# Short SSM products that wait in the plan while many TensorE instructions were begun lately, and a new stretch ahead of the first exponential

## The chip, the cores and the metric

The kernel runs on one core of one Trainium2 chip. The metric is the device time of one execution in microseconds (us), the median of several runs. Engines are named as the profile names them: PE is TensorE (PEld its weight loads), DVE is VectorE, ACT is ScalarE, POOL is GpSimd, SP is SyncE, from which most transfers are issued.

## What is computed

Two independent layers on sequences of 2048 rows with 640 features; their outputs are joined along the features.

```python
def _A_ref(x, Lambda_re, Lambda_im, B_re, B_im, C_re, C_im, log_dt, Dskip):
    Lam = Lambda_re + 1j * Lambda_im
    dt = jnp.exp(log_dt)
    Lam_bar = jnp.exp(dt * Lam)
    B_bar = ((Lam_bar - 1.0) / Lam)[:, None] * (B_re + 1j * B_im)
    Bu = jnp.einsum("bld,pd->blp", x + 0j, B_bar)
    for t in range(L):
        h = Lam_bar[None, :] * h + Bu[:, t, :]
        hs.append(h)
    return 2.0 * jnp.einsum("blp,dp->bld", jnp.stack(hs, 1), C_re + 1j * C_im).real + x * Dskip

def _B_ref(x, wq, wk, wv, wo):            # 32 query heads of 20, one key and value head
    q = (x @ wq).reshape(B, S, 32, 20).transpose(0, 2, 1, 3)
    scores = jnp.einsum("bhqd,bkd->bhqk", q, x @ wk) * (20 ** -0.5)
    o = jnp.einsum("bhqk,bkd->bhqd", softmax(scores, axis=-1), x @ wv)
    return o.transpose(0, 2, 1, 3).reshape(B, S, 640) @ wo
```

The first layer is a state space model (SSM), a recurrence over time with a complex diagonal; the second is attention with 32 heads that share one key and one value head.

## The kernel before

**The program is planned when it is built.** `Schedule` holds a small model of the five engines. Each step is an `Op` with an engine, a planned duration, its dependencies and a priority. Whenever a modelled engine is free, `pick` takes the ready step with the lowest priority number, and the order in which steps were picked becomes each engine's instruction stream; `Emitter` adds the semaphore waits. A `gate` is a function that must be true for a step to be picked. Nothing of the planner runs on the chip, but each of its rules decides the fixed order there. A random seed (`SEEDS`) shifts the due places of the background tasks, and `STAGES` changes the planner's constants as tiles are filled.

**Attention.** The scores of one head and 512 queries against 128 keys make a tile, [128 keys, 512 queries]; 32 blocks of 64 tiles are 2048 tiles. PSUM has eight banks of [128, 512]: two groups of three (`SC`) and two single ones (`MB`). `fill` scores two or three tiles into an SC group, and one ACT exponential (L1530) turns two or three of them into bf16 probabilities in `PR`. If the third bank holds a tile of the other route, DVE takes it: a `TENSOR_SCALAR` to int16 (L867), an exponential by its bits, and three shifted copies of it by POOL (`int64_add`, L1858) or DVE; four value products with differently scaled values (`VS`) then stand for one. Such tiles (here: tiles of the DVE route) are also scored into MB banks when one is free. The two SC groups take turns: while ACT reads one, PE fills the other, which it may do once ACT and DVE have emptied it (`slot_last`). The value products (L1946) add up in one MB bank, `pvbank`.

**Background work** shares PE with that: query projections, output projections (`WO`), and the SSM: unit tasks (`xaT` with `BA`, `BT`), a scan on DVE, and the output products `y_task`, whose moving operand has 512 columns, or 128 for the last 128 features (`k == 4`) and for the skip term (`diagD`). `ride` hands these to PE in steps of up to 256 columns, each product as four matmuls on 32 columns of the array; `board` lets one product that is cut in row groups ride along with a score fill.

**Ahead of the first exponential.** x is loaded plainly for the first 1024 rows and transposed by PE (`turn`), and loaded transposed for the others (`XB`: pieces of 128-feature columns on SP, one of five, then three and two columns). `kv` makes the keys of each 512 rows on PE (L1162, with `wks`, the key weights repeated four times), the largest absolute key (L1168) and the scaled keys `KT`. `bound` makes the largest of all (L1194) and `M0`, a matrix that turns absolute queries into a bound on each query's scores; `qt_task` makes the first queries, the product with `M0`, and `QT` (L867). `attention` starts when all SC banks are free. `v_task` makes the values (L1218) and casts them (L1226).

**At the end** tiles of the DVE route are taken until `LAST` tiles before the end and copied by POOL until `POOL_LAST` tiles before it.

## Time and profile before

| what | us |
|---|---|
| median of 3 runs | 697.55 (697.17 to 698.18) |
| the profiled execution | 697.62 |
| its span, first to last instruction | 695.9 |
| start of the first exponential | 18.41 |
| end of the last exponential | 687.68 |
| PE, ACT, DVE, POOL busy | 683.2, 681.8, 637.0, 470.4 |

The profile is of one execution. A row of a timeline has the start, the length, the engine, the line, the operation with what it writes and reads, and how many instructions it joins; in brackets, the idle time just before it and what ended that. "issue" there means that no semaphore ended it. A row of the groups ends with the busy time, the mean of one in ns, and the idle time before the group. A row of windows has a stretch, then for PE, PEld, DVE, ACT and POOL the busy time and the number of instructions, the granted clock of TensorE as a share of full speed, and the share and rate of the transfers. A row of waits has who waited for whom, the total, how often, and the longest.

### The profile page before, as it was taken

What the parts mean: (1) busy time and instruction counts of PE and PEld (TensorE: products, weight loads), DVE (VectorE), ACT (ScalarE), POOL (GpSimd) and SP (SyncE); (2) the same over time, 40 slices, a digit from 0 to 9 for tenths busy, and PEclk for the clock granted to TensorE, in tenths of its full rate; (3) what the DMA queues carried; (4) which work ended last, traced back from release to release, by engine and by line L of the source; (5) the groups of instructions that cost most, each with busy time, mean ns of one, the idle gap of its engine ahead of it and who ended that gap; (6) DMA issues with size and microseconds to landing.
All of it is one profiled execution on the core that took longest, in us unless ns stands there. A gap on an engine that the chain in (4) does not pass through costs nothing.

```text
span 695.9 us, 27390 instructions
## 1 busy us (share of the span) xinstructions
PE 683.2 (98%) x11488; PEld 250.6 (36%) x11490; DVE 637.0 (92%) x1243; ACT 681.8 (98%) x703; POOL 470.4 (68%) x796
## 2 busy tenths in 40 slices
PE   8999999999999999999999999999999999999998
PEld 5322332334334333333433333334333332343335
DVE  7899999999999889999999999999999999977795
ACT  7999999999999999999999999999999999999996
POOL 4256666564587668767778777676776767788880
DMA  9659641211130111102110101131000001110001
GB/s 217 175 127 187 139 103 39 62 26 32 30 94 13 32 27 27 35 21 29 44 26 22 28 27 28 35 58 20 13 15 12 20 15 36 37 29 22 21 15 41
DMA packets 77591, 34.48 MB, mean 50 GB/s; under 512 B 58350, under 2 KB 77470, under 8 KB 77470
## 3 DMA queue, kind: packets, MB, share of 16 engines
q1 hardware_dynamic: 76650, 32.57, 20.3%
q8 instruction: 92, 1.51, 0.9%
q10 hardware_dynamic: 820, 0.16, 0.1%
q14 instruction: 29, 0.24, 0.1%
HBM read 11.53 MB, written 9.75 MB: 31 GB/s over the span
## 4 chain that ended last, share of the span: by engine, by line
PE 56%; ACT 42%; DVE 1%; issue 0%
ACT PR L1530 41%; PE MB L1946 21%; PE MB L800 14%; PE SC L1626 10%; PE MB L810 8%; PE MB L730 1%; DVE BIG L867 1%; PE SC L1162 1%; PE SC L726 1%; PE MB L726 0%; ACT L2197 0%; PE SC L730 0%; DVE pvsb L1925 0%; PE MB L1279 0%; DVE QT L867 0%
## 5 line engine op out<-in xcount | busy, mean ns | idle before, releaser
L1530 ACT ACTIVATE PR<-SC 128x1024 bf16<-128x1024 f32 (+1 forms) x678 | 666.6, 1131 | 4.5 <-PE SC L1626 3.3
L1858 POOL INT64_ADD BIG<-BIG x761 | 458.1, 617 | 198.1 <-DVE BIG L867 54.7
L867 DVE TENSOR_SCALAR BIG<-SC 128x512 int16<-128x512 f32 x560 | 376.2, 684 | 38.7 <-PE SC L1626 33.1
L1946 PE MATMUL MB<-BIG,VS 128*32 128x512 bf16 (+1 forms) x2468 | 269.8, 376 | 1.2 <-DVE pvsb L1925 0.9
L1626 PE MATMUL SC<-QT,KT 32*128 32x512 bf16 (+1 forms) x2073 | 265.3, 378 | 4.4 <-ACT PR L1530 1.8
L1946 PE MATMUL MB<-PR,VP 128*32 128x512 bf16 (+1 forms) x1495 | 222.3, 378 | 0.1
L1626 PEld LDWEIGHTS SC<-QT,KT 32*128 32x128 bf16 x2073 | 67.3, 91 | 133.8 <-ACT PR L1530 77.1
L1946 PEld LDWEIGHTS MB<-BIG,VS 128*32 128x32 bf16 x2468 | 68.5, 95 | 65.5 <-issue 41.4
L1946 PEld LDWEIGHTS MB<-PR,VP 128*32 128x32 bf16 x1495 | 55.1, 94 | 45.8 <-issue 33.0
L867 DVE TENSOR_SCALAR BIG<-BIG 128x1024 int16<-128x1024 int16 (+1 forms) x136 | 52.3, 419 | 0.9 <-PE MB L1946 0.4
L800 PE MATMUL MB<-CA,W 128*32 128x320 bf16 (+2 forms) x992 | 51.4, 299 | 0.4 <-DVE BIG L2366 0.4
L810 PE MATMUL MB<-xaT,BT 32*128 32x256 bf16 x192 | 37.1, 273 | 0.0
L800 PE MATMUL MB<-CT,W 128*32 128x512 bf16 (+1 forms) x640 | 36.0, 302 | 0.6 <-issue 0.6
L800 PE MATMUL MB<-xaT,BA 128*32 128x256 bf16 x800 | 31.8, 275 | 0.0
L810 PE MATMUL MB<-diagD,xaT 32*128 32x128 bf16 x320 | 31.3, 217 | 0.0
L810 PEld LDWEIGHTS MB<-diagD,xaT 32*128 32x128 bf16 x320 | 17.7, 92 | 29.1 <-ACT PR L1530 17.7
L800 PEld LDWEIGHTS MB<-CA,W 128*32 128x32 bf16 x992 | 22.8, 96 | 14.2 <-issue 5.7
L800 PE MATMUL MB<-xaT,BT 128*32 128x256 bf16 x608 | 26.2, 274 | 0.0
L2133 DVE CAST stg<-MB 128x512 bf16<-128x512 f32 x35 | 23.8, 680 | 1.8 <-PE MB L800 1.1
L862 DVE TENSOR_TENSOR prod<-MB,tab 128x1024 bf16<-128x1024 f32 x20 | 24.3, 1215 | 0.2
L867 DVE TENSOR_SCALAR BIG<-MB 128x512 int16<-128x512 f32 x35 | 23.8, 679 | 0.6 <-PE MB L1626 0.6
L2406 DVE TENSOR_TENSOR_SCAN g<-sc,hst,prod 128x256 bf16<-128x256 f32 x30 | 22.5, 749 | 0.0
(178 smaller groups left out, 502.4 us busy)
## 6 DMA issues: line engine op xcount, KB each, us to landing
out_dram<-stg SPq DMA_DIRECT2D x33, 128.0 KB, 2.0
qd<-BIG SPq DMA_DIRECT2D x20, 128.0 KB, 2.1
QT<-qd SPq DMA_DIRECT2D x28, 80.0 KB
OP<-pvsb SPq DMA_DIRECT2D x105, 20.0 KB
rdP<-recs SPq DMA_DIRECT2D x105, 20.0 KB
lbd<-BA SPq DMA_DIRECT2D x5, 320.0 KB, 2.7
CT<-in_B_x_dram SPq DMA_DIRECT2D x2, 640.0 KB, 5.3
BA<-in_A_B_re_dram SPq DMA_DIRECT2D x1, 800.0 KB, 7.5
```

The costliest lines, as they stand in the source:

```text
L726: r = e.matmul(out[32 * j:32 * j + 32], lhsT=lhsT[:, 32 * j:32 * j + 32], rhs=rhs, start=start, stop=stop, tile_position=(0, 32 * j), skip ...
L730: return lambda e: e.matmul(out, lhsT=lhsT, rhs=rhs, start=start, stop=stop, **kw)
L800: x = e.matmul(out[32 * j:32 * j + 32], lhsT=lhsT[:, 32 * j:32 * j + 32], rhs=rhs, start=start, stop=r.end is tag, tile_position=(0, 32 * ...
L810: return lambda e: e.matmul(out, lhsT=lhsT[at], rhs=rhs[at], start=start, stop=r.end is tag, tile_position=(32 * row, 0), skip_group_check ...
L862: return lambda e: e.tensor_tensor(out, a, b, op)
L867: return lambda e: e.tensor_scalar(out, a, s1, s2, op0=op0, op1=op1)
L1530: ex = self.act(lambda e: e.activation(dst, t[:, 0:512 * n], ACT.Exp, scale=1.0 / UNIT), 0.8333 * 512 * n + 64, table="exp", deps=[op], re ...
L1626: r = e.matmul(out[:, bank.off + lo:bank.off + lo + n], lhsT=p.KT[32 * j:32 * j + 32, 128 * c:128 * c + 128], rhs=p.QT[32 * j:32 * j + 32, ...
L1858: op.fns.append(lambda e: e.int64_add(words(dst), words(src), add))
L1946: r = e.matmul(bank.tensor[32 * j:32 * j + 32, bank.off + at:bank.off + at + n], lhsT=v[:, c, 0:32], rhs=rhs[:, lo:lo + n], start=first an ...
L2133: ev = self.dve(lambda e: e.tensor_copy(st, bank.ap), 645, deps=[prev], reads=[bank.key], writes=[key], prio=self.EV, gate=(lambda: last.e ...
L2406: o = self.dve(lambda e, ri=ri, init=init: e.tensor_tensor_scan(p.g[:, u, ri, :], rdec, p.prod[:, 1, 0, ri, :], init, ALU.mult, ALU.add), ...
```

## The change

Two things are added to the planner, one stretch is rewritten, and the plan is drawn anew.

**A gate on short products.** Every PE step that is begun is noted with its number of instructions (two for each entry in its list, eight for a ridden product, which is four matmuls with four weight loads). A ridden step whose moving operand has at most 128 columns may be picked only if fewer than `FETCH` = 220 instructions were begun in the last `SUPPLY` = 3400 planned ns; else it is asked again 130 ns later.

```diff
+    def issued(self, span):
+        while self.issues and self.issues[0][0] < self.t - span:
+            self.issues.popleft()
+        return sum(n for _, n in self.issues)
...
+            self.issues.append((self.t, op.per * len(op.fns)))
...
+    SUPPLY, FETCH = 3400.0, 220.0
...
-                         load=n, writes=[bank.key], hook=hook, gate=lambda: bool(r.steps))
+                         load=n, writes=[bank.key], hook=hook, gate=lambda: bool(r.steps) and (
+                             r.steps[0][0][0][2].shape[-1] > 128 or self.s.issued(self.SUPPLY) < self.FETCH or bool(self.s.at(self.s.t + 130.0))))
+            op.per = 8
```

On PE, within an output task with 128 columns of the SSM (`CT`, `CA` and `diagD` are its weights, `W` the states; SC<-QT,KT is a score fill, MB<-PR,VP and MB<-BIG,VS are value products), before:

```order
L810 MATMUL MB<-diagD,xaT 128x128 x3
L800 MATMUL MB<-CT,W 32x128 x4
L800 MATMUL MB<-CA,W 32x128 x4
L800 MATMUL MB<-CT,W 32x128 x4
L800 MATMUL MB<-CA,W 32x128 x4
L800 MATMUL MB<-CT,W 32x128 x4
L800 MATMUL MB<-CA,W 32x128 x4
L800 MATMUL MB<-CT,W 32x128 x4
L800 MATMUL MB<-CA,W 32x128 x4
L810 MATMUL MB<-diagD,xaT 128x128
L1626 MATMUL SC<-QT,KT 128x512 x3
```

and with the change, in the same task:

```order
L820 MATMUL MB<-diagD,xaT 128x128 x3
L810 MATMUL MB<-CT,W 32x128 x4
L810 MATMUL MB<-CA,W 32x128 x4
L1992 MATMUL MB<-PR,VP 32x512
L1992 MATMUL MB<-BIG,VS 32x512 x5
L1992 MATMUL MB<-PR,VP 32x512
L1992 MATMUL MB<-BIG,VS 32x512
L820 MATMUL MB<-diagD,xaT 128x128
L1672 MATMUL SC<-QT,KT 128x512 x3
```

After eight short products two of them stand between two fills here, and eight value products of 512 columns in the place of the others.

**The third bank.** When the third bank of an SC group holds a tile that DVE will, in the plan, empty too late, the next fill of that group takes two tiles and does not wait for it (`third_limit`, `third_known`, `third_late`, and `skip` in `fill`).

```diff
+        if self.skip[i]:
+            n, third = min(n, 2), self.third[i]
+            self.n_skip += 1
...
-        self.slot_last[i] = [ex] + first
+        self.slot_last[i] = [ex] + first + ([third] if third is not None else [])
+        self.third[i] = first[0] if first else third
...
+        ex, other = self.slot_last[i][0], self.slot_last[1 - i][0]
+        return ex.start + ex.dur + (other.dur if other.eng == "act" else 0.0) - 522.0 + self.SKIP
```

**The stretch ahead of the first exponential.** The last key product is no longer cut in two halves. The transposed pieces are of five, four and one column. M0 is made in two steps: from the first three maxima on ACT, then, as the smaller (more negative) of that and the last one, on DVE. DVE instead of ACT copies `wks`; the keys of the first two row groups are scaled on DVE, the others on ACT. The value products wait for M0's product, in the third banks, and attention starts without waiting for these banks.

```diff
-    WKP, QUAD_KEYS, WKE = 0.9, 0, "a"
-    TURNED, KEYS = ("adada", "adada"), "adaa"
-    XB = ((2, 0, 5, 11250.0), (3, 0, 3, 12500.0), (3, 3, 5, 13400.0))
+    WKP, QUAD_KEYS, WKE = 0.9, 0, "d"
+    TURNED, KEYS = ("adada", "adada"), "ddaa"
+    XB = ((2, 0, 5, 11250.0), (3, 0, 4, 13350.0), (3, 4, 5, 14150.0))
...
-            m = self.dve(lambda e: e.tensor_reduce(out=p.mab[:, 5:6], in_=p.mab[:, 0:5], axis=AX.X, op=ALU.max), 120,
-            self.m0_op = self.dve(self.ts(p.M0[:], p.mask0[:], p.mab[:, 5:6], None, ALU.mult), 200, port=True,
+            m = self.act(lambda e: e.activation(p.M0[:].rearrange("p a b -> p (a b)"), p.mask0[:].rearrange("p a b -> p (a b)"), ACT.Copy,
+                                                scale=p.mab[:, 4:5]), 260,
+            yield lambda: 3 in self.red_op
+            self.m0_op = self.dve(lambda e: e.scalar_tensor_tensor(out=p.M0[:], in0=p.mask0[:], scalar=p.mab[:, 3:4], in1=p.M0[:],
+                                                                   op0=ALU.mult, op1=ALU.min), 250, port=True,
...
-                           gate=lambda: self.lively(self.V_BY[tb // 3]))
+                           gate=lambda: (tb > 1 or self.m_first is not None and self.m_first.start is not None and (tb == 0 or self.tile_n > 0)) and self.lively(self.V_BY[tb // 3]))
...
-        mine = [b for _, bs in self.slots for b in bs]
+        mine = [b for _, bs in self.slots for b in bs[:-1]]
```

On PE, from the key products (SC<-BIG,wks) to the first scores, before; MB<-BIG,wqp are the first queries, MB<-PR keeps PE busy, MB<-BIG,M is the product with M0, SC<-wvr,BIG are the values, and the one row SC<-BIG is a product that rides ahead of the first scores:

```order
L1279 MATMUL MB<-BIG,wqp 128x512 x5
L1162 MATMUL SC<-BIG,wks 128x512 x8
L1162 MATMUL SC<-BIG,wks 128x256 x4
L730 MATMUL MB<-PR 128x512
L1218 MATMUL SC<-wvr,BIG 128x20 x20
L730 MATMUL MB<-PR 128x512 x2
L730 MATMUL MB<-BIG,M 32x512 x4
L1218 MATMUL SC<-wvr,BIG 128x20 x20
L730 MATMUL MB<-PR 128x512 x2
L810 MATMUL SC<-BIG 128x512
L1626 MATMUL SC<-QT,KT 128x512 x4
```

and with the change:

```order
L1294 MATMUL MB<-BIG,wqp 128x512 x5
L1171 MATMUL SC<-BIG,wks 128x512 x10
L737 MATMUL MB<-PR 128x512 x5
L737 MATMUL MB<-BIG,M 32x512 x4
L1235 MATMUL SC<-wvr,BIG 128x20 x20
L1672 MATMUL SC<-QT,KT 128x512 x4
```

Both groups of value products stood ahead of the first scores, with the rider; now one group does, behind M0's product, and the first scores have no rider.

**The plan.** `SEEDS` goes from 169732 to 531817, some constants of `STAGES` change, `LAST` goes from 12 to 16 and `POOL_LAST` from 14 to 29. On PE, the last rows of the program (SC<-BT,pvsb and SC<-WO,OP are parts of the last output projection), before:

```order
L726 MATMUL SC<-BT,pvsb 32x128 x16
L726 MATMUL MB<-BT,pvsb 32x512 x4
L726 MATMUL SC<-BT,pvsb 32x512 x8
L726 MATMUL SC<-WO,OP 32x512 x16
L726 MATMUL SC<-BT,pvsb 32x512 x8
```

and with the change:

```order
L733 MATMUL SC<-WO,OP 32x512 x8
L733 MATMUL SC<-BT,pvsb 32x128 x16
L733 MATMUL MB<-BT,pvsb 32x512 x4
L733 MATMUL SC<-WO,OP 32x512 x8
L733 MATMUL SC<-BT,pvsb 32x512 x8
```

Eight of the sixteen products of the last step stand ahead of the last value rows now.

129 lines of the change are left out of this document (76 added, 53 removed).

## The prediction

> **What bounds the kernel.** I read the page first: the busy shares, then the group of the exponentials.
>
> ```profile
> span 695.9 us, 27390 instructions
> PE 683.2 (98%) x11488; PEld 250.6 (36%) x11490; DVE 637.0 (92%) x1243; ACT 681.8 (98%) x703; POOL 470.4 (68%) x796
> L1530 ACT ACTIVATE PR<-SC 128x1024 bf16<-128x1024 f32 (+1 forms) x678 | 666.6, 1131 | 4.5 <-PE SC L1626 3.3
> ```
>
> TensorE (PE) and ScalarE (ACT) are both at 98%. A busy PE is a modelled figure, so I ask ACT: 678 exponentials, with only 4.5 us of idle time before them. Then the groups kept apart by shape, and ACT's timeline in order of time, in which a row ends where ACT waited visibly (a row bears the shape of its first instruction and counts both shapes).
>
> ```profile
> L1530 ACT ACTIVATE PR<-SC 128x1024 bf16<-128x1024 f32 x579 | 544.7, 1068 | 4.3 <-PE SC L1626 3.3 <-PE MB L1626 0.3 <-PE MB L1946 0.2
> L1530 ACT ACTIVATE PR<-SC 128x1536 bf16<-128x1536 f32 x98 | 141.6, 1505 | 0.1
> 18.41 185.56 ACT L1530 ACTIVATE PR<-SC 128x1024 bf16<-128x1024 f32 x183 [1.81 <-PE SC L1626]
> 204.13 133.17 ACT L1530 ACTIVATE PR<-SC 128x1024 bf16<-128x1024 f32 x136 [0.15 <-PE MB L1626]
> 337.93 35.60 ACT L1530 ACTIVATE PR<-SC 128x1024 bf16<-128x1024 f32 x37 [0.63 <-PE SC L1626]
> 373.70 132.75 ACT L1530 ACTIVATE PR<-SC 128x1024 bf16<-128x1024 f32 x137 [0.17 <-PE MB L1626]
> 506.64 19.42 ACT L1530 ACTIVATE PR<-SC 128x1024 bf16<-128x1024 f32 x20 [0.20 <-PE SC L1626]
> 526.30 46.90 ACT L1530 ACTIVATE PR<-SC 128x1024 bf16<-128x1024 f32 x48 [0.24 <-PE SC L1626]
> 573.37 108.38 ACT L1530 ACTIVATE PR<-SC 128x1024 bf16<-128x1024 f32 x112 [0.17 <-PE MB L1946]
> 682.14 5.54 ACT L1530 ACTIVATE PR<-SC 128x1024 bf16<-128x1024 f32 x5 [0.39 <-PE SC L1626]
> 687.05 0.63 ACT L1530 ACTIVATE PR<-SC 128x512 bf16<-128x512 f32 x1
> 511.75 9.29 ACT L1530 ACTIVATE PR<-SC 128x1024 bf16<-128x1024 f32 x10
> 520.79 1.18 ACT L1530 ACTIVATE PR<-SC 128x1024 bf16<-128x1024 f32 x1
> 167.86 8.25 ACT L1530 ACTIVATE PR<-SC 128x1536 bf16<-128x1536 f32 x6
> 169.19 1.55 ACT L1530 ACTIVATE PR<-SC 128x1536 bf16<-128x1536 f32 x1
> ```
>
> So the span is three pieces: 18.41 us until the first exponential, 669.27 us of exponentials (18.41 to 687.05 + 0.63), 8.2 us after them. The last four rows give the undisturbed step: ten 1024-column exponentials from 511.75 to 520.79 are 0.904 us each, a 1536-column one from 167.86 to 169.19 is 1.33 us. Then 579 x 0.904 + 98 x 1.33 + 0.63 = 654.4 us is what ACT must do, and 669.3 - 654.4 = 14.9 us is lateness of the scores, which sits in ACT's way whatever else is busy. Only part of it is visible as a gap: seven gaps after the first make 1.95 us, and each costs 0.16 more than it shows, since an exponential takes 1.068 but the next may begin after 0.904; that is 3.1 us. The other 11.8 us are delays too short to part two exponentials.
>
> **The work on ACT.** The order of the changed program holds 582 exponentials of two tiles, 99 of three and none of one, against 579, 98 and 1 (681 and 678 instructions): 1461 tiles instead of 1453. Eight tiles fewer take the VectorE route (587 against 595). The step per tile from the rows above is 1.33 - 0.904 = 0.426 us, so 3 x 0.904 + 1.33 - 0.48 = **+3.6 us** (the one-tile step is 0.904 - 0.426 = 0.48). Nothing hides that: ACT is the chain. VectorE and GpSimd are relieved, and neither bounds the span.
>
> **The stretch ahead of the first exponential.** The chain of waits there, from the timeline:
>
> ```profile
> 7.97 0.11 PEld L1162 LDWEIGHTS SC<-BIG,wks 128*128 128x128 bf16 x2 [1.05 <-ACT wks L1047]
> 9.74 1.41 PEld L1162 LDWEIGHTS SC<-BIG,wks 128*128 128x128 bf16 x8
> 9.97 1.67 PE L1162 MATMUL SC<-BIG,wks 128*128 128x512 bf16 x7 [0.16 <-issue]
> 14.26 0.34 PEld L1162 LDWEIGHTS SC<-BIG,wks 128*128 128x128 bf16 x4 [0.31 <-DMA BIG<-in_B_x_dram]
> 13.84 0.69 DVE L1168 TENSOR_REDUCE mab<-SC 128x1 f32<-128x512 f32 x1
> 15.91 0.29 DVE L866 TENSOR_SCALAR M<-mask,mab 128x128 bf16<-128x128 f32 x1
> 16.25 0.40 PE L730 MATMUL MB<-BIG,M 128*32 128x512 bf16 x4
> 16.70 0.81 DVE L867 TENSOR_SCALAR QT<-MB,lift 128x512 bf16<-128x512 f32 x1 [0.51 <-PE MB L730]
> 17.43 0.38 DVE L1226 CAST VP<-SC 128x80 bf16<-128x80 f32 x2
> 17.98 0.58 PE L1626 MATMUL SC<-QT,KT 32*128 32x512 bf16 x4
> ```
>
> The last transposed piece of x lands at 14.26; four short key products, two maxima, a maximum of maxima, M0 (ready 16.20), its product, QT (ready 17.51). The scores start only at 17.98, since a rider in their first operation needs the bank that the value cast empties (17.43 + 0.38 = 17.81). The change leaves one 512-column product behind the last landing, one maximum (0.69), and one operation that makes M0 from a part made earlier; and it runs the value products after M0's product, so that bank is free. From the landing: 14.26 + 0.38 product + 0.2 to VectorE + 0.69 + 0.06 + 0.29 (M0, by the row of the old M0) = 15.88; the product at 15.93, QT 16.38 to 17.19, scores 17.24, first exponential 0.43 later (as 17.98 to 18.41): 17.67, or -0.74 us. The other end is PE's own order: 24 whole key and query products at (1.67 - 0.38) / 6 = 0.215 us each now stand between the start of that run and the last maximum, so with a start at 9.74 as before the last begins at 9.74 + 23 x 0.215 = 14.69, 0.43 after the landing: -0.31 us. The start comes earlier, since wks is now copied on VectorE ahead of its casts and the 1.05 us wait for ACT shrinks; I take **-0.6 us**. The second transpose now brings four columns and the third one, with the same total behind the same queue, so I leave the last landing where it was; had the split of the pieces delayed it by 0.3, the term would be -0.4. The maximum for the rows that are loaded back, and the stores of q that now stand behind a transposed load on SP, are for blocks 2 and up: over a hundred tiles of exponentials (some 50 us) cover them.
>
> **The pauses of PE.** What the gate on short products is aimed at:
>
> ```profile
> 333.30:336.40 3.10, 3.10 (x154) 2.47 (x157) 2.97 (x8) 3.10 (x5) 1.85 (x4) 1.00 0.49 102
> 336.40:337.30 0.90, 0.28 (x24) 0.11 (x15) 0.85 (x2) 0.90 (x1) 0.57 (x1) 1.00 0.00 0
> 337.26 0.24 PE L800 MATMUL MB<-CT,W 128*32 128x128 bf16 x4 [0.61 <-issue]
> q8 instruction: 92, 1.51, 0.9%
> ```
>
> In 3.1 us PE began 154 products and 157 weight loads, then stood for 0.6 us waiting for nothing that a semaphore shows, and the exponential at 337.93 came 0.63 late. PE ran out of instructions: queue 8 brings them, 1.51 MB in 92 packets, 16 KB each. The changed order breaks such runs at about 110 products per four score fills (22 stretches above 130 before, 3 now). [...]
>
> The second cause is the third bank of a score group, which VectorE empties:
>
> ```profile
> PEld SC L1626 <- DVE BIG L867: 31.3, 77, 0.7
> 203.68 0.10 PEld L1626 LDWEIGHTS SC<-QT,KT 32*128 32x128 bf16 x3 [0.42 <-DVE BIG L867]
> 373.25 0.10 PEld L1626 LDWEIGHTS SC<-QT,KT 32*128 32x128 bf16 x3 [0.42 <-DVE BIG L867]
> 525.86 0.10 PEld L1626 LDWEIGHTS SC<-QT,KT 32*128 32x128 bf16 x3 [0.42 <-DVE BIG L867]
> ```
>
> Each of the last three stands half a microsecond ahead of a visible gap (204.13, 373.70, 526.30). The change fills two tiles there and leaves the third bank to VectorE. So of the seven gaps five are addressed: 0.63, 0.15, 0.17, 0.24 and, with the ending rearranged, 0.39; with 0.16 each that is 2.4 us. Of the 11.8 us of short delays I take a fifth (31.3 us of the idle time before score weights is VectorE's, against 77.1 that ends with ACT itself and is harmless): 2.1 us. Together **-4.5 us**, between 0 and about -9. The gate is the planner's: on the chip no instruction waits for longer, other products just stand where the short ones stood. What waits is the short products' bank, which their output task holds longer, so fewer tiles of the VectorE route find one (28 instead of 35 are scored into such banks); that price is in the +3.6.
>
> **The end.** After the last exponential the chain goes through this:
>
> ```profile
> 690.14 0.42 DVE L862 TENSOR_TENSOR pvsb<-pvsb,SC 128x256 bf16<-128x256 bf16 x1 [0.54 <-PE SC L730]
> 691.50 1.03 PE L726 MATMUL SC<-WO,OP 128*32 128x512 bf16 x16
> 693.02 0.60 ACT L2126 ACTIVATE PR<-SC 128x512 bf16<-128x512 f32 x1 [0.70 <-PE SC L726]
> ```
>
> Of the 16 products at 691.50, four at a time in 0.215 us, eight now stand earlier: -0.43 us. The last exponential is one of three tiles, with six products behind it instead of two, in the shadow of output products; between +0.3 and -0.5 for that, taken as 0: **-0.4 us**.
>
> **Sum.** +3.6 - 0.6 - 4.5 - 0.4 = -1.9 us on the profiled execution, 695.9 to 694.0 of span. That execution took 697.62 us in all (1.7 us around the span), the median of the runs is 697.55: **695.6 us**. Faster or slower here means by over 0.2%, 1.4 us, about what a measurement of this kernel tells from none.
>
> **Rivals.** (1) The eight tiles are paid and the lateness stays: spread-out products meet the same fills elsewhere. For it: PE is at 98%, and 11.8 of the 14.9 us are delays behind ordinary products. Against: 24 fewer value products. +3.6 - 0.6 - 0.4 = 2.6: 700.2 us, slower; it decides once less than 1.2 us of lateness is won back. (2) The visible gaps alone are won: 2.6 - 2.4 = +0.2: 697.8, no change. (3) The rearranged order removes twice what I take, as nearly all lateness passes through PE's order, which is made anew: 2.6 - 9 = -6.4: 691.2. (4) The gate does not do what it says, since instructions are not what PE lacked at 336.4: then that gap stays (0.63 + 0.16), 695.6 + 0.8 = 696.4. It would need another cause without a semaphore, which no row names. [...]
>
> **Chances.** The forecast 0.47, (1) 0.18, (2) 0.20, (3) 0.10, (4) 0.05. Faster than 696.15: 0.47 + 0.10 = 0.57; within: (2) and (4), 0.25; slower than 698.95: 0.18. The likeliest case's own range is 693.5 to 697.5; to hold 8 in 10 it goes from 692.3 into the slower case, 699.8.
>
> **What would show it.** The first exponential near 17.8 us, its scores no longer behind a value cast; 681 exponentials; a late time (stretch less 0.904 and 1.33 per exponential) near 10.4 us; no pause of PE above 0.5 us "issue" in the products of W; fewer score fills behind VectorE than 77; about 7.8 us after the last exponential. I am wrong if the late time stays near 15 us, or if the first exponential comes after 18.4.

## The result and the profile after

| | before | after |
|---|---|---|
| median, us | 697.87 (697.04 to 698.37, 6 runs) | 701.16 (700.10 to 702.21, 6 runs) |
| ratio | | 1.0047 [1.0034, 1.006] |
| the profiled execution, us | 697.62 | 702.21 |

The change makes the kernel slower, by 3.3 us in the medians, where 1.9 us less was forecast, and 701.16 lies above the range. The page of the changed kernel, its span, busy shares and the group of the exponentials:

```profile
span 700.5 us, 27323 instructions
PE 685.4 (98%) x11479; PEld 251.3 (36%) x11479; DVE 634.3 (91%) x1227; ACT 685.5 (98%) x705; POOL 468.1 (67%) x794
L1575 ACT ACTIVATE PR<-SC 128x1024 bf16<-128x1024 f32 (+1 forms) x681 | 671.0, 1127 | 5.7 <-PE SC L1672 4.7
```

Three more exponentials, and the idle time ahead of them went from 4.5 to 5.7 us. ACT's timeline shows where:

```profile
18.12 12.02 ACT L1575 ACTIVATE PR<-SC 128x1024 bf16<-128x1024 f32 x13 [1.54 <-PE SC L1672]
31.01 2.07 ACT L1575 ACTIVATE PR<-SC 128x1024 bf16<-128x1024 f32 x2 [0.87 <-PE SC L1672]
34.01 1.02 ACT L1575 ACTIVATE PR<-SC 128x1024 bf16<-128x1024 f32 x1 [0.93 <-PE SC L1672]
35.32 58.51 ACT L1575 ACTIVATE PR<-SC 128x1024 bf16<-128x1024 f32 x59 [0.29 <-PE SC L1672]
94.24 355.52 ACT L1575 ACTIVATE PR<-SC 128x1024 bf16<-128x1024 f32 x357 [0.41 <-PE SC L1672]
450.20 158.05 ACT L1575 ACTIVATE PR<-SC 128x1024 bf16<-128x1024 f32 x163 [0.43 <-PE SC L1672]
608.49 84.80 ACT L1575 ACTIVATE PR<-SC 128x1024 bf16<-128x1024 f32 x86 [0.24 <-PE SC L1672]
697.47 0.60 ACT L2172 ACTIVATE PR<-SC 128x512 bf16<-128x512 f32 x1 [1.20 <-PE SC L733]
```

All the visible gaps that the prediction named (204, 338, 374, 526, 682 us) are gone: between 94.24 and 449.76 no exponential is visibly late. In their place stand six: three at 31 to 36 us, where the kernel before had none, with 2.09 us together, and one each at 94, 450 and 608 us, with 1.08 together. The four terms of the prediction, read off both profiles (late time is the stretch of exponentials less 0.904, 1.33 or 0.48 us for each, the last one included, which puts the kernel before at 15.0 in the place of 14.9; "again" is a second profile of the changed kernel, first of the experiments below):

| us | before | after | again | forecast of the change |
|---|---|---|---|---|
| first exponential begins | 18.41 | 18.12 | 18.15 | -0.6 |
| work of ACT (tiles) | 654.2 (1453) | 657.8 (1461) | 657.8 | +3.6 |
| late time | 15.0 | 17.4 | 15.3 | -4.5 |
| of it until 45 us | 0.3 | 3.0 | 1.8 | |
| after the last exponential | 8.2 | 7.2 | 7.1 | -0.4 |
| span | 695.9 | 700.5 | 698.3 | -1.9 |

Three terms have the forecast sign, the work the forecast size. The fourth failed: in sum no lateness was won, and some was added.

### The profile page after: what moved, and what is told of

It is laid out like the page before. It is cut to its first block, busy times and chain, and to the rows that moved or that the text cites. A ratio compares the mean times of both kernels' runs of the same rounds, so it can differ in the third digit from the quotient of the medians.

```text
span 700.5 us, 27323 instructions
## 1 busy us (share of the span) xinstructions
PE 685.4 (98%) x11479; PEld 251.3 (36%) x11479; DVE 634.3 (91%) x1227; ACT 685.5 (98%) x705; POOL 468.1 (67%) x794
## 4 chain that ended last, share of the span: by engine, by line
PE 56%; ACT 36%; DVE 3%; DMA 2%; SPq 2%; issue 1%; POOL 0%
ACT PR L1575 36%; PE MB L1992 21%; PE MB L810 15%; PE SC L1672 10%; PE MB L820 8%; DMA BA<-in_A_B_im_dram 2%; SPq L722 1%; DVE BIG L877 1%; PE SC L733 1%; PE MB L733 0%; POOL BIG L1904 0%; PE MB L737 0%; PE SC L810 0%; SPq L718 0%; DVE g L2452 0%
## 5 line engine op out<-in xcount | busy, mean ns | idle before, releaser
L1992 PE MATMUL MB<-BIG,VS 128*32 128x512 bf16 (+1 forms) x2412 | 266.1, 378 | 0.6 <-DVE pvsb L1971 0.4
L1992 PE MATMUL MB<-PR,VP 128*32 128x512 bf16 (+1 forms) x1509 | 217.6, 378 | 0.0
L1992 PEld LDWEIGHTS MB<-BIG,VS 128*32 128x32 bf16 x2412 | 66.6, 95 | 65.5 <-issue 37.6
L810 PE MATMUL MB<-CA,W 128*32 128x320 bf16 (+2 forms) x992 | 53.6, 300 | 0.1
L877 DVE TENSOR_SCALAR BIG<-BIG 128x1024 int16<-128x1024 int16 (+1 forms) x126 | 47.5, 413 | 1.4 <-PE MB L1992 1.0
L820 PE MATMUL MB<-xaT,BT 32*128 32x256 bf16 x184 | 35.6, 272 | 0.7 <-ACT PR L1575 0.7
L810 PEld LDWEIGHTS MB<-CA,W 128*32 128x32 bf16 x992 | 22.9, 96 | 13.4 <-issue 5.2
L810 PEld LDWEIGHTS MB<-xaT,BA 128*32 128x32 bf16 x800 | 17.5, 96 | 11.6 <-issue 9.7
```

Of the source, the lines that this page charges most:

```text
L810: x = e.matmul(out[32 * j:32 * j + 32], lhsT=lhsT[:, 32 * j:32 * j + 32], rhs=rhs, start=start, stop=r.end is tag, tile_position=(0, 32 * ...
L820: return lambda e: e.matmul(out, lhsT=lhsT[at], rhs=rhs[at], start=start, stop=r.end is tag, tile_position=(32 * row, 0), skip_group_check ...
L877: return lambda e: e.tensor_scalar(out, a, s1, s2, op0=op0, op1=op1)
L1992: r = e.matmul(bank.tensor[32 * j:32 * j + 32, bank.off + at:bank.off + at + n], lhsT=v[:, c, 0:32], rhs=rhs[:, lo:lo + n], start=first an ...
```

## The experiments

Three questions: is ACT's work really paid in full; what makes the new wait near 31 us; and what are the 15 us of lateness, if not what the gate and the third-bank rule remove? The terms of ten of the profiles (the ratio is to runs of the kernel before on the same chip, in bold what the text below is about):

| kernel | first exp. | tiles | late time (until 45 us) | after the last exp. | span | ratio |
|---|---|---|---|---|---|---|
| the change again | 18.15 | 1461 | 15.3 (1.8) | 7.1 | 698.3 | 1.0030 [1.0018, 1.0042] |
| change, scalings of B later | 17.97 | 1461 | **19.2 (4.6)** | 7.3 | 702.3 | 1.0082 [1.007, 1.0094] |
| change, x pieces cut as before | 17.98 | 1461 | 15.0 (0.75) | 7.5 | 698.2 | 1.0018 [1.0009, 1.0027] |
| change, no gate | 18.13 | 1462 | **19.1 (3.3)** | **9.2** | 704.6 | 1.0097 [1.0081, 1.0114] |
| change, no third-bank rule | 18.21 | 1463 | 17.9 (1.6) | 7.9 | 702.6 | 1.0079 [1.0064, 1.0094] |
| before with the gate | 18.33 | 1457 | 15.0 (0.5) | 9.0 | 698.3 | 1.0021 [1.0011, 1.0031] |
| before with another seed | 18.84 | 1452 | 17.2 (0.3) | 8.5 | 698.4 | 1.0021 [1.0011, 1.0032] |
| before, one dense run spread | 19.54 | 1453 | 14.4 | 7.9 | 696.0 | 0.9993 [0.9985, 1.0002] |
| before, that and earlier evictions | 18.45 | 1453 | 16.1 | 8.2 | 697.0 | 0.9993 [0.9984, 1.0002] |
| before, eight exponentials twice | 18.30 | **1469** | 15.9 | 7.9 | 703.6 | 1.0118 [1.0104, 1.0132] |

### The same kernel again (a_again)

No edit.

> The changed kernel as it is, profiled once more. If the wait of VectorE for the load of BA at 26 to 28 us belongs to the order (theory L), this execution shows it too: a gap of 0.8 us or more ahead of an exponential near 31 us, and a time of 700 to 702.5. If it was a chance of one execution (rival), the gap is missing and the profiled execution is near 699.

Median 700.14 us against 698.28, so 1.9 us slower where the first measurement had 3.3. The late time until 45 us differs by 1.2 us between the two profiles of one kernel; ACT's timeline of this one:

```profile
31.35 416.28 ACT L1575 ACTIVATE PR<-SC 128x1024 bf16<-128x1024 f32 x419 [1.18 <-PE SC L1672]
```

The first gap is here too and the two behind it are not: from 31.35 to 447.63 us ACT is never visibly idle. But 350 of these 419 exponentials are of two tiles and 69 of three, so 350 x 0.904 + 69 x 1.33 = 408.2 us of work took 416.3: 8 of the 15.3 us of late time lie in a row without a gap. The delay of one exponential is the time from the start of the one before it, less that one's step. Sorted by size, past 45 us, in us: delays of 200 ns or more fell from 5.33 (before) to 2.73, those of 100 to 200 ns rose from 2.40 to 3.68, and the smaller ones stayed, 6.83 and 6.87.

### The new wait near 31 us (a_split, a_load_later)

The chain of it in the profile after, from the timelines of PE, DVE and SP:

```profile
3.23 9.37 SPq L722 DMA_TRANSPOSE BIG<-in_B_x_dram  x3
14.40 0.53 SPq L718 DMA_DIRECT2D BA<-in_A_B_im_dram  x1
27.84 0.55 DVE L877 TENSOR_SCALAR CA<-BA,sc 128x1280 bf16<-128x1280 bf16 x1 [1.73 <-DMA BA<-in_A_B_im_dram]
29.51 0.68 DVE L1335 CAST BIG<-SC 128x512 bf16<-128x512 f32 x1
30.24 0.40 PE L810 MATMUL SC<-BIG 128*32 128x512 bf16 x4 [1.04 <-DVE BIG L1335]
```

and the same two issues before, with the same scaling:

```profile
3.21 8.38 SPq L715 DMA_TRANSPOSE BIG<-in_B_x_dram  x3
13.43 0.65 SPq L711 DMA_DIRECT2D BA<-in_A_B_im_dram  x1
28.00 0.55 DVE L867 TENSOR_SCALAR CA<-BA,sc 128x1280 bf16<-128x1280 bf16 x1
```

The three transposes keep SP for 9.37 us instead of 8.38. The last two of them bring the same five columns, but cut four and one they take 2.75 + 1.26 us to issue, and cut three and two 1.45 + 1.54. All loads behind them go out 1 us later, among them the imaginary part of the SSM's input matrix (`BA`), which takes 13.4 us to land (13.1 before) and so comes at 27.8 us. On DVE the scaling of `BA` waits 1.73 us, the cast of the next queries stands behind it in the program's order, PE stands 1.04 us behind the cast, and a score fill behind that. Then something else comes on top, seen in a table of windows (length, then busy time and number of instructions of PE, PEld, DVE, ACT and POOL, granted clock, share and rate of the transfers):

```profile
29.20:30.24 1.04, 0.00 (x2) 0.00 (x0) 0.99 (x4) 0.94 (x2) 0.00 (x0) 1.00 0.29 2
30.24:31.24 1.00, 1.00 (x15) 0.32 (x15) 0.79 (x4) 0.23 (x1) 0.00 (x0) 1.00 0.22 64
31.24:35.00 3.76, 3.76 (x37) 0.74 (x29) 3.17 (x8) 2.81 (x3) 0.00 (x0) 0.55 0.97 229
35.00:38.00 3.00, 3.00 (x39) 0.74 (x36) 2.68 (x7) 2.71 (x4) 0.00 (x0) 1.00 1.10 221
```

PE was idle for 1.04 us, ran for one, and then had a clock of 0.55 for 3.76 us, which made the two further gaps at 34 and 35 us. In the second profile of the same kernel PE was idle for 1.34 us of 29 to 31 us, the clock stayed at 1.00, and those two gaps are missing: that is the 1.2 us between them.

Two experiments. The first cuts the pieces three and two again, as in the kernel before, with the plan's order untouched:

```diff
+        a, b = (next(o for o in order if o.dma_key == k) for k in ("xb30", "xb34"))
+        for o, lo, hi in ((a, 0, 3), (b, 3, 5)):
+            to, src = self.xbT[:, lo:hi, 1536:2048], self.B_x[0, 1536:2048, 128 * lo:128 * hi]
+            o.fns = [lambda e, to=to, src=src: e.dma_start_transpose(to, src)]
```

> The changed kernel with the last two transposed pieces of x cut as before, three columns and two instead of four and one; no instruction changes its place and nothing is left out. The cut costs SyncE 1.04 us of issue (2.68 + 1.26 against 1.45 + 1.45), and every load behind it is as much later. Theory L: BA lands 1.0 to 1.4 us earlier (near 26.8), VectorE's wait of 2.04 shrinks to 1 us or less, the exponential at 31.35 is late by 0.5 at most instead of 1.39, and the kernel takes 0.8 to 1.4 us less than the changed one's 700.1: 698.7 to 699.4. Rival (the tail of that load does not hang on its issue): no change.

Its timelines:

```profile
8.59 3.04 SPq L586 DMA_TRANSPOSE BIG<-in_B_x_dram  x2
13.58 0.67 SPq L726 DMA_DIRECT2D BA<-in_A_B_im_dram  x1
26.57 0.55 DVE L885 TENSOR_SCALAR CA<-BA,sc 128x1280 bf16<-128x1280 bf16 x1
20.13 71.12 ACT L1583 ACTIVATE PR<-SC 128x1024 bf16<-128x1024 f32 x73 [0.22 <-PE SC L1680]
```

The load goes out at 13.58 and lands 12.3 us later, the scaling waits for nothing, and from 20.13 to 91.25 us there is no gap: late time until 45 us falls to 0.75. The first exponential does not come later for it (17.98). The ratio goes from 1.0030 to 1.0018; the two intervals overlap from 1.0018 to 1.0027, so the timeline carries this, not the ratio. The wait is made by the cut, and it is 1 to 2 us of the loss; most of the loss is not in it.

The second leaves the cut and moves the two waiting scalings behind the casts in DVE's order:

```diff
+        mine = [i for i, o in enumerate(order) if o.eng == "dve" and "bn0_0" in o.reads]
+        a, b, to = mine[:3]
+        moved = [order[a], order[b]]
...
+        return order[:a] + [o for o in order[a + 1:to] if o not in moved] + moved + order[to:]
```

> The changed kernel with two operations alone moved: the first two scalings of BA stand on VectorE behind the two casts and the copy that they stood ahead of; every other instruction keeps its place, and nothing is left out. Theory L (the late load blocks VectorE's queue, the query cast behind it keeps TensorE idle, and the idle time halves the granted clock): no gap at 31 to 36 us, no clock of 0.50 there, and 1.0 to 2.7 us less than the changed kernel, 698.4 to 700. Rival (the eight tiles and an unchanged lateness are all of it): less than 0.5 us.

It became slower, 704.01 us:

```profile
31.18 0.33 DVE L882 TENSOR_TENSOR Mm<-maskM,mcol 128x160 bf16<-128x160 f32 x1 [1.97 <-DMA mcol<-mrep]
36.01 0.69 DVE L1345 CAST BIG<-SC 128x512 bf16<-128x512 f32 x1
36.85 0.39 PE L1682 MATMUL SC<-QT,KT 32*128 32x512 bf16 x3 [2.39 <-DVE BIG L1345]
37.28 1.02 ACT L1585 ACTIVATE PR<-SC 128x1024 bf16<-128x1024 f32 x1 [2.27 <-PE SC L1682]
```

Now DVE waits 1.97 us for the next late transfer (`mcol`, which SP issues behind `BA`), the scalings pile up behind it, and the cast that PE needs comes at 36.01: PE stands 2.39 us where it stood 1.04. The wait was moved, not removed; moving one consumer was no cure here, where two loads (`BA` and `mcol`) were late in one queue.

### Is ACT's work paid in full? (b_eight_more)

In the kernel before, eight two-tile exponentials are done twice, each right behind the first time:

```diff
+    TWICE = (60, 110, 160, 210, 260, 310, 360, 410)
...
+            again = Op("act", o.fns, o.dur, reads=o.reads, writes=o.writes)
```

> The kernel before with eight exponentials of two tiles executed twice, the second behind the first by a wait of ScalarE on itself; nothing else moves. It measures the price of work on ScalarE: if ScalarE sets the end with all of it (theory T, on which the 3.6 us for eight more tiles rest), each costs a whole step of 0.904 us and its wait, 8 x 0.9 to 1.1 = 7.2 to 8.8 us. If the lateness of the scores takes part of it up (rival: an exponential that begins late only because TensorE is behind is not made later), 2 to 5 us.

```profile
L1542 ACT ACTIVATE PR<-SC 128x1024 bf16<-128x1024 f32 (+1 forms) x686 | 674.7, 1131 | 4.4 <-PE SC L1638 3.0
```

706.63 us against 698.36: 8.3 us for eight, 1.03 each, the whole length of one (0.904, and a late time that rose by 0.9). The lateness did not shrink to make room: ACT's idle 4.4 us are not a reserve that added work fills.

### The gate (b_gate, a_no_gate, b_spread, products_alone)

The gate alone in the kernel before:

```diff
+    SUPPLY, FETCH = 3400.0, 220.0
...
+            op.per = 8
```

> The kernel before with the rule on short products alone; the order is drawn anew. Theory G (the rule wins the pauses of TensorE for want of instructions, 0.8 to 1.5 us, and the loss comes from the other parts): 696 to 697, no issue gap in the products of W. Theory D (a rule that holds products back makes the planner draw another order, in which the scores are as late as before or later): 698 or more, with the issue gap gone all the same.

The pause at 336.4 us is gone and the late time is 15.0, as without the gate. The end became 0.8 us longer and four more tiles came to ACT (1.7 us by 0.426 each): 699.70 us against 698.28, slower.

The change without its gate:

```diff
-    SUPPLY, FETCH = 3400.0, 220.0
+    SUPPLY, FETCH = 3400.0, 1e9
```

> The changed kernel with the limit of the rule on short products set out of reach; the order is drawn anew. Theory G: 1 us or more above the changed kernel, with issue gaps above 0.5 us back in the products of W. Theory D: up or down by 1 to 4 us with lateness in other places, the pauses making 1.5 us of it at most.

704.67 us. This order has the densest runs of all, 173 products in 3.4 us, and yet no pause of PE without a releaser in them. It is slower by a late time of 19.1 and an end of 9.2, with a clock of 0.50 from 31 to 34 us, behind the same wait. Within the changed rules the gate thus goes with a faster plan, and within the old rules with a slower one: the plan is drawn anew either way, and what the gate itself does is not seen in these two.

So the one dense run was spread by hand in the kernel before: the same 24 pairs of ridden products, two or three between two fills and a group of value products with them, where there were four or five, everything else in place:

```diff
+        take = (2, 3, 3, 2, 3, 3, 3, 2, 3, 0)
...
+        for i in range(10):
+            new += [pairs.pop(0) for _ in range(take[i])]
+            if values and (i > 0 or not fills):
+                new.append(values.pop(0))
+            if fills:
+                new.append(fills.pop(0))
```

> The kernel before with one stretch alone put in another order: between 331.4 and 339 us the 24 short products of W on TensorE, three or two instead of five between two score fills, alternate with value products that stood behind them; all else keeps its place, nothing is left out. Theory S (TensorE stops at 336.4 because it began 311 instructions in 3.1 us and the next had not been brought): no pause above 0.3 us there, the exponential at 337.9 not late, 0.4 to 0.9 us won: 697.2 to 697.7 beside 698.0. Rival (something else stops TensorE at that time): the pause of 0.6 us stays at the same time or the same instruction.

Its windows where the pause was (columns as above), and a row of PE's timeline further on:

```profile
333.30:336.40 3.10, 3.10 (x105) 1.81 (x102) 3.10 (x8) 3.10 (x4) 1.87 (x4) 1.00 0.67 155
336.40:339.50 3.10, 3.10 (x104) 1.70 (x100) 2.87 (x7) 3.10 (x4) 2.07 (x4) 1.00 0.00 0
```

```profile
482.04 0.29 PE L834 MATMUL MB<-BIG,xaT 128*32 128x128 bf16 x8 [0.39 <-issue]
```

207 and 204 instructions in 3.1 us where there were 311, PE busy throughout, and the exponential that was 0.63 late on time. But at 482 us, in another dense run, a pause of 0.39 without a releaser stands where the profile before shows none. The spreading need not have made it, for the same product pauses where nothing was spread, with eight exponentials twice:

```profile
488.44 0.29 PE L812 MATMUL MB<-BIG,xaT 128*32 128x128 bf16 x8 [0.37 <-issue]
```

It is the same instruction of PE's order in both (15637 recorded products and weight loads stand ahead of it); in the profile before PE stands 0.11 us there, and in the order with earlier evictions 0.66. Such pauses thus belong to places of the order, and their length to the execution. Late time is 0.6 lower, the median 0.35 us, within what can be told from none. That bounds what the gate could win at 336.4: 0.8 us (0.63 + 0.16) if nothing were given back.

What PE can be supplied with was measured by itself, with stages of products (columns, groups of four) on PE alone and nothing else of the kernel:

```diff
+STAGES = ((512, 100), (128, 400), (512, 40), (256, 200), (512, 40), (128, 40), (512, 40))
...
+            for n, count in STAGES:
+                for k in range(count):
+                    for j in range(4):
+                        r = e.matmul(ps[k % 2][32 * j:32 * j + 32, 0:n], lhsT=w[:, 32 * j:32 * j + 32], rhs=x[:, 0:n], start=True,
```

> Left out: all of the computation; TensorE alone begins products of 32 weight columns and 512, 128, 512, 256, 512, 128 and 512 columns on zeros, four at a time, 100, 400, 40, 200, 40, 40 and 40 times, with no wait between them. Theory S: the 1600 products of 128 columns with their weight loads (3200 instructions) outrun what brings them, so after some 300 instructions pauses of 0.3 to 1 us come again and again, and the stretch takes clearly longer than 400 x 0.055 = 22 us; at 256 columns (73 instructions in a microsecond) few pauses or none. Rival: no pause at 128 columns.

```profile
29.32 1.97 PE L63 MATMUL ps<-x,w 128*32 128x128 bf16 x128 [1.06 <-issue]
33.05 1.97 PE L63 MATMUL ps<-x,w 128*32 128x128 bf16 x128 [1.76 <-issue]
...
66.33 2.61 PE L63 MATMUL ps<-x,w 128*32 128x128 bf16 x128 [1.48 <-issue]
70.06 41.71 PE L63 MATMUL ps<-x,w 128*32 128x512 bf16 x1280 [1.12 <-issue]
```

In a long run of 128-column products PE works for 1.97 us and then stands until 3.7 us have passed on average, again and again: 128 products and their 128 weight loads each time, so 256 instructions per (66.33 - 29.32) / 10 = 3.70 us, 69 per us. The stages behind it (1280 products in 41.71 us) are of 512, 256 and again 512 columns, with 160 of 128 columns at their end, and have no pause: the wide products show none, in a stretch with 61 instructions per us (2560 in 41.71 us), and its short run of narrow ones passes too, with a pause of 0.55 only behind it. The packets of queue 8, which the page calls instruction, are in the traces too: behind each of these pauses PE goes on 1.3 to 1.5 us after one of 16 KB has landed, and so it does in the kernel (1.6 us at 337.26 in the kernel before, 1.4 us at 482.04 with the run spread, 1.6 us at 488.44 above). So the prediction's cause of the pause at 336.4 holds, with a size: 311 instructions in 3.1 us, 100 per us, is more than what arrives, while 207 in 3.1 us, 67 per us, is not. Whether a dense run of some 3 us pauses should then depend on what had arrived ahead of it, and 173 products in 3.4 us could pass; this was not tested by itself.

### Fewer products (b_fewer_products, b_groups_out)

If the lateness comes from a full PE, it must fall when PE gets less to do. In the kernel before, two of the four value products are left out of every second group; then, in another kernel, every second group of four is replaced by one product of 32 columns. Both leave out part of the sums of the attention.

```diff
+            if o.eng == "pe" and len(o.fns) == 4 and ("VS" in o.reads or "VP" in o.reads) and o.start > 60000.0:
+                n += 1
+                if n % 2:
+                    del o.fns[2:]
```

> The kernel before; left out: of every second group of four value products from 60 us on, two of the four; the order and all else stay. TensorE has about 60 us of products less to do. Theory P (the scores are late because TensorE stands in other products when a score bank comes free, so lateness hangs on how full it is): the late time of the exponentials falls from 15 us to 8 or less, 690 to 692. Rival (the short delays come from the scores' own chain of ScalarE, VectorE and banks): it stays above 12 us.

```profile
PE 681.2 (98%) x10548; PEld 249.4 (36%) x10548; DVE 636.8 (92%) x1243; ACT 680.6 (98%) x703; POOL 469.0 (68%) x796
```

940 products fewer and PE is busy as before (683.2): the four products of a group lie on different columns of the array and run side by side (in the kernel before one group begins at 482.00 and 482.01 us, 0.39 us each, and the next at 482.22), so in this trace two cost what four do. This one did not take the load away; its late time was 12.8, its time 695.98 us in one run (698.94 before). Why 2.2 us of lateness went all the same stays open; other profiles of the order before, with small edits, have 14.4 to 16.1. Hence the other:

```diff
+                if n % 2:
+                    o.fns = [lambda e: e.matmul(bank[0:32, 0:32], lhsT=self.VZ[:], rhs=self.KT[:, 0:32], start=False, stop=False,
```

> The kernel before; left out: from 60 us on, every second group of four value products (473 groups), with one product of 32 columns in the place of each; the order, the waits and all else stay. Unlike two products of the four, which stream side by side, a whole group gives TensorE its 0.2 us back, some 90 us in all. Theory P (scores are late because TensorE stands in other products when a score bank comes free): the late time falls from 15.2 to 8 us or less, about 690 in all. Rival (the delays come from the scores' own chain of ScalarE, VectorE and banks): it stays above 11 us.

```profile
PE 622.5 (90%) x10061; PEld 240.6 (35%) x10063; DVE 634.7 (91%) x1243; ACT 680.2 (98%) x703; POOL 468.7 (68%) x796
```

PE has 61 us less to do by the profile, 473 groups of four, and a late time of 13.2 is left. Of it 3.4 lies at 513 to 536 us, where the kernel before has 0.6 and where PE's clock was halved twice (513.6 to 517.0 and 527.3 to 534.1 us; its mean over the run is 0.993). Taking the 2.7 more out, 10.5 is left: by this one profile some 4.5 of 15 us go with PE's load, the others do not. Of the 4.5, 2.6 are delays of up to 100 ns, which fell from 6.8 to 4.3. The time was 696.12 us in one run, beside 698.85 of the kernel before.

### The third-bank rule, the seed, and DVE (a_no_skip, b_seed, b_in_place)

The change without the rule that lets a fill skip the third bank:

```diff
-        return o is not None and (o.start is None or self.s.seen(o, "pe") > max(self.third_limit(i), self.s.t))
+        return False
```

> The changed kernel without the rule that fills two tiles when the third bank is late; the order is drawn anew. Theory K (that rule alone takes lateness behind VectorE away): the lateness behind VectorE back from 1.26 to 2 us or more, 0.8 to 1.5 us slower by that alone. Theory D (the draw decides): the total lateness outside 26 to 37 us between 13 and 17 us either way, and the time within 699 to 706 with no sign of its own.

704.05 us; late time 17.9, 2.6 above the second profile of the change; its 1463 tiles are 0.9 us more of work (2 x 0.426), and the end is 0.8 longer. The fills behind DVE are as many as in the kernel before:

```profile
PEld SC L1672 <- DVE BIG L877: 32.3, 77, 0.8
```

To size that, the kernel before with nothing but another seed:

```diff
-    SEEDS, REPLAYS = (169732,), 12
+    SEEDS, REPLAYS = (1740,), 12
```

> The kernel before with no rule and no number of the planner changed but the seed of its random choices. Theory D (each new draw of the order costs or gains some microseconds whatever the rule does): 1 to 4 us away from before, 699 to 702, with a lateness of 14 to 18 us in other places and a work of ScalarE that differs by some tiles. Rival (an order drawn by the same rules is as good): within 0.7 us.

700.35 us against 698.94: drawn anew, the same rules come out 1.0021 [1.0011, 1.0032] slower, by a late time of 17.2 instead of 15.0. So a difference of two or three us between two plans says little about the rule that differs. What the rule is worth stays open within that. One sign is for it: the delays of 200 ns and more past 45 us sum to 2.7 to 4.1 us in the profiles with the rule (two plans) and to 4.3 to 6.8 in the complete kernels without it (four plans and edits of one of them).

Last, the remaining delays behind DVE in the kernel before, without drawing anew: two evictions of third banks are placed ahead of three other DVE operations (65.7 and 522 us), two products of the scan of 1.2 us are cut in halves with an eviction between (201 and 369 us), and the dense run is spread as above.

```diff
+        for at, count in ((65688.0, 3), (522278.0, 3)):
...
+            order = order[:to] + [o] + order[to:i] + order[i + 1:]
+        for at in (201060.0, 368991.0):
...
+            one, two = self.halves[id(o)]
+            rest = Op("dve", [two], o.dur / 2, reads=o.reads, writes=["prod0b"])
```

> The kernel before with five places put in another order and nothing drawn anew: the short products of W spread as before (331 to 339 us); two evictions of a third score bank on VectorE put ahead of three copies each (65.7 and 522 us); and two products of 1.2 us on VectorE that stand ahead of such an eviction (201 and 369 us) cut in halves with the eviction between them. Nothing is left out. Theory O (the large delays behind VectorE sit in single places of the order and are won there one by one, when the rest is left as it is): the exponentials at 67.4, 204.1, 373.7 and 526.3, late by 256, 356, 320 and 502 ns, are late by less than 150 each, the lateness falls by 1.4 to 2 us, 696.3 to 697.3 beside 698.4. Rival (an eviction that comes sooner makes the next one late): the lateness stays within 0.8 us of 15.2 less the 0.7 of the spread products, 697.5 to 698.5.

```profile
202.64 0.68 DVE L934 TENSOR_SCALAR BIG<-SC 128x512 int16<-128x512 f32 x1
203.24 0.68 DVE L929 TENSOR_TENSOR prod<-MB,tab 128x512 bf16<-128x512 f32 x1
204.14 0.10 PEld L1693 LDWEIGHTS SC<-QT,KT 32*128 32x128 bf16 x3 [0.42 <-DVE prod L929]
204.59 25.45 ACT L1597 ACTIVATE PR<-SC 128x1024 bf16<-128x1024 f32 x26 [0.15 <-PE MB L1693]
```

The eviction ran earlier, and now the fill waits for the second half of the scan's product instead: the gap of 0.15 us is there again, at 204.59 instead of 204.13. The delays at 374 and 527 us stayed too, the one at 67.4 grew from 256 to 564 ns (67.8), and a new one of 768 came at 230.7. 697.54 against 697.81, no difference that can be told. DVE is busy without a gap in the 2 us ahead of the places at 204, 374 and 527 us, in both orders: it has more to do there than time.

## Why the prediction was wrong, point by point

**The work on ACT, +3.6: right.** 681 exponentials, 1461 tiles, and the eight doubled exponentials show that each is paid with its whole length. The reason given for the eight tiles is not: the gate alone kept all 35 tiles that are scored into MB banks, and the change without its gate had 30 of them (28 in the change). In orders drawn with 40 other seeds (counted in the plan, nothing run), the rules of before give some 1455 tiles in the mean, those of the change 1462, either the new stretch ahead of the first exponential or the new `STAGES` numbers alone some 1468, and these two together 1460, so their prices do not add up. The change also moves three due places that its description leaves unnamed (`CB_FROM`, `CB_STEP`, `Y_STEP`). None of that was run, and which part costs the tiles stays open.

**The first exponential, -0.6: right in sign, in this pair near the other end.** The chain in the profile after:

```profile
13.87 0.76 PEld L1171 LDWEIGHTS SC<-BIG,wks 128*128 128x128 bf16 x5 [0.62 <-DMA BIG<-in_B_x_dram]
15.16 0.69 DVE L1177 TENSOR_REDUCE mab<-SC 128x1 f32<-128x512 f32 x1 [0.51 <-PE SC L1171]
15.96 0.35 DVE L1210 SCALAR_TENSOR_TENSOR M<-mask,mab,M 128x128 bf16<-128x128 f32 x1
16.82 0.81 DVE L877 TENSOR_SCALAR QT<-MB,lift 128x512 bf16<-128x512 f32 x1 [0.44 <-PE MB L737]
17.69 0.40 PE L1672 MATMUL SC<-QT,KT 32*128 32x512 bf16 x4 [0.32 <-DVE QT L877]
```

One maximum, one operation for M0, QT at 17.63 and the scores at 17.69 with no rider ahead of them: that is the forecast chain. But its start is not the last landing. The four-column piece came at 13.87, and four more whole products at 0.215 us each put the last one at 14.73, just the other end that the prediction worked out (-0.31) and set aside. Measured -0.29 between the two profiles. The start scatters, though: the profile before and the five of the table with the old stretch have it at 18.30 to 19.54, 18.65 in the mean, the profile after and the five with the new one at 17.97 to 18.21, 18.09 in the mean: 0.56 apart by the means, 0.31 by the medians, so the size stays open between the two ends.

**The pauses of PE: cause right, price nearly nothing.** The dense runs are short of instructions, and the isolated products and the spread run speak against rival (4), which denied it: alone, PE works through blocks of 256 instructions and stands for 1.5 to 2.0 us between two of them, one block every 3.70 us in the mean, and with 207 instructions in 3.1 us in the place of 311 the pause is gone. Yet in this kernel the pause at 336.4 cost 0.8 us at most, and with its run spread another dense run paused. The gap at 682 us, which the prediction put down to the ending, begins with such a pause too, in value products, which the gate does not hold back:

```profile
681.12 0.63 PE L1946 MATMUL MB<-BIG,VS 128*32 128x256 bf16 x13 [0.34 <-issue]
```

**"Together -4.5 us": the step that failed.** The prediction took five visible gaps with 0.16 each (2.4) and a fifth of the short delays (2.1; a fifth of 11.8 is 2.4) off, and put nothing on. The first part came: past 45 us delays of 200 ns and more fell by 2.6 us in the second profile (2.0 in the first). The second did not: a new plan brings its own delays of 100 to 200 ns, 1.3 us more of them, and as many smaller ones as before. Past 45 us the late time went from 14.7 to 13.5 (again) and 14.4 (after): 0.3 to 1.2 us won instead of 4.5. The waits that the rule is to remove were fewer in this plan:

```profile
PEld SC L1672 <- ACT PR L1575: 81.5, 200, 1.0
PEld SC L1672 <- DVE BIG L877: 26.9, 64, 0.8
PEld SC L1672 <- issue: 16.9, 48, 0.4
```

64 fills behind DVE instead of 77, and 4.4 us less of it; but 4.4 us more behind ACT (77.1 before) and 2.2 more without a releaser (14.7). It looks as if the wait for the bank ended sooner and the next one ended last. But that the rule did it is not shown by these counts: without it there are 77 again, yet the change without its gate, which keeps the rule, has 86, and the old rules with another seed 84. Against the 15 us the runs leave no single cause: some 4.5 go with PE's load in the one profile that took it away, 2.2 more came with the other seed, a part sits where DVE has more work than time (the three places near 204, 374 and 527 us), and the rest is open. The 6.8 us in delays of up to 100 ns were hardly touched by anything that only drew the plan anew or moved operations (6.2 to 7.2 in all of these profiles); only the two kernels with fewer products on PE have less of them (5.8 and 4.3).

**The new wait: not priced at all.** "I leave the last landing where it was" looked at x only. That a transposed piece of four and one costs SP 1 us more than three and two, that all loads behind go out later, and that DVE waits for one of them at 27.8 us with PE's next cast behind it, was a term of +1.5 to +2.7 us; the median lies 1.4 us above the upper bound. The row was there: `BA` lands 13.1 us after its issue at 13.43, so at 26.5, 1.5 us ahead of the scaling at 28.00 that the kernel before does with it; the change used up that slack at both ends.

**The end, -0.4: right in sign,** and larger: -1.0 and -1.1 measured.

Summed on the profiled executions: -0.3 + 3.6 + 2.4 - 1.0 = +4.7 (695.9 to 700.5), and -0.3 + 3.6 + 0.3 - 1.1 = +2.5 for the second profile (698.3). This is rival (1), tiles paid and lateness stays, which gave 700.2 and got 0.18 of the chance; the two medians lie 1 us above it (701.16) and at it (700.14), with a new wait that it does not have and an end that was shorter. Its row, "11.8 of the 14.9 us are delays behind ordinary products", was the better guide. None of the versions run is shown to be faster than the kernel before; the two that changed its order in place (0.9993 each) cannot be told from it.

## What to carry to other kernels

Work on the engine that sets the end was paid in full (8.3 us for eight exponentials more); lateness that is spread over hundreds of short delays was not won back by removing the few visible gaps (0.3 to 1.2 us instead of 4.5), since a new order brought as many of its own: book the first in full, and the second only for delays whose successor is named. Before a plan with a random part is judged, draw the old rules again with another seed: here one other seed alone was 0.21%, as much as the gate alone. When transfers of one queue are cut anew, follow every load behind them to the instruction that uses it, and look what stands behind that one on its engine.

## What the runs showed of the hardware

- Instructions reached PE at 69 per us in a long run of 128-column products with a weight load each: 256 instructions every 3.70 us, 1.97 us of work and 1.5 to 2.0 us of standing still. PE went on 1.3 to 1.5 us after a packet of 16 KB had landed on queue 8.
- A halved clock of PE came behind 0.49 to 2.39 us of idle time, but not each time. In the changed kernel 1.04 us at 29.20 was followed by a clock of 0.55 for 3.76 us, that is half speed for (1 - 0.55) / 0.5 x 3.76 = 3.4 us (0.50 in every stretch between 32.00 and 34.50); in the second profile a wait of the same kind (1.34 us idle in 29 to 31 us) left it at 1.00. Half clock also came behind 1.17 us (the change without its gate, 0.50 from 31 to 34 us) and 2.39 us (scalings later, 0.55 in the mean from 37 to 40 us), and, with the groups left out, behind 0.49 us of idle time in 3.40 (510.2 to 513.6). What decides it is not shown.
- Issuing a transposed load of 512 rows took SP 1.26 us for one column of 128 features, 1.54 for two, 1.45 for three and 2.68 to 2.75 for four.
- The real part of the SSM's matrix landed 7.6 us after its issue and the imaginary part, of the same 800 KB and issued 0.57 us later, 13.4 us:

```profile
BA<-in_A_B_re_dram SPq DMA_DIRECT2D x1, 800.0 KB, 7.6
BA<-in_A_B_im_dram SPq DMA_DIRECT2D x1, 800.0 KB, 13.4
```

- Four products on 32 columns each cost PE what two do, when they are issued as one group: 940 fewer changed its busy time, whose ends are modelled, from 683.2 to 681.2 us.
